# Where weight conversions stand behind attention, which queue stores a group's last piece, a lag ahead of a group, and a fill split unevenly

## The chip, the core and the metric

The kernel runs on one core of one Trainium2 chip. Its engines are TensorE (PE), VectorE (DVE), ScalarE (ACT), GpSimd (POOL) and SyncE (SP, which issues DMAs). The metric is the time of one execution on the device, in microseconds; less is better.

## What is computed

Three stages follow each other, all in float32. A gated linear attention runs over 4 batches, 8 heads, 768 steps and head size 48, with a complex decay a per step and channel. Its output rows go through a top-1 mixture of 8 experts, and the result through a dense gated stage.

```python
scale = min(mag, 0.999) / (mag + 1e-6)           # mag = |a|
for t in range(768):                             # S is complex, 48 x 48 per head
    S = (a[t] * scale[t]) * S + outer(k[t], v[t])
    y[t] = q[t] @ S.real
x = y as 3072 rows of 384
e = argmax(x @ w_gate); x = gate * (relu(x @ w1[e]) @ w2[e])
out = ((x @ v1) * (x @ v2)) @ w3 @ w_out         # v1, v2, w3, w_out arrive as float64
```

## The kernel before

**Attention in chunks.** The 768 steps are 3 groups of 4 chunks of 64 steps. One chunk of one pair of batches is a unit `u = (g, q, c)`, so a group has 8 units. Work of the attention runs as two streams of Python generators. `first()` (`Attn.elementwise`) goes through 24 pieces, on DVE and ACT for the most part: it takes the loaded decays, makes the prefix products of the decays (L891, L893) and multiplies q and k by them (`L923`, the last DVE operation of a piece). The result is stored to a scratch tensor in HBM, `qkd`, through POOL's queue. For the last piece of a group (pieces 9, 17 and 23) the first 64 lanes go through SP's queue and the other 64 through POOL's (L931, L932). `second()` (`Attn.groups`) reads `qkd` back by unit (tile `kk`, L1025 on SP), which can start only when the whole group has been stored.

**A unit.** `scores` transposes q and k on PE (L1009), copies the transposes with ACT (`qkT`, L1010), multiplies them (L1037) and masks the product with DVE (`at`, L1041). `outputs` makes the unit's 64 rows from the masked scores and the state (L1056, L1057), copies them (`xo`, L1060), and every two or four such tiles `route` computes the experts' logits and scatters the rows with POOL (L162). `chain` carries the state `W` in PSUM from unit to unit. Its first part multiplies the carried state by a permutation (L1094) and copies the sum as `z` with ACT (L1095); its second part adds the unit's outer products (L1101), scales the result with 8 ACT operations and one DVE operation into `cb` or `cc` (L1108, L1109) and with one more DVE operation in place (L1110). The next unit's L1094 needs both.

**The filling.** After each of the two parts of `chain` the generator calls `fill(cost)`, which takes steps of `scores`, `outputs` and `route` from a pool until their planned prices add up to `cost`. Prices are planned nanoseconds: 430 for four transposes, 680 for half the scores, 650 for two heads of outputs. Both calls use `FILL = 2600`.

**What sets the order.** `drive` interleaves the two streams by a planned clock for each: whichever is behind goes next, and what the second stream yields is multiplied by `GM = 0.85`. The order in which instructions are traced is their priority. A scheduler then plays the program with durations of its own, and lets an engine take a later instruction when the earlier one is not ready in that play. The order on each engine is fixed then; on the chip each engine takes its instructions strictly in that order. `tc.issue_after(x)` adds an edge: what is traced inside the block on x's engine stands behind x.

**The conversions.** The dense stage's last two matrices are float64. `Fuse` loads them (tile `fdr`, L291, on SP), splits each into a high and a low half on DVE and ACT (`halves`, L322 to L339) and multiplies them. While group 2's units are traced, one conversion step is taken after each `fill`, two after every third. They cover the 8 pieces of `w_out` and 4 of 8 blocks of `w3`. Each step is ordered behind `S.end` on S.end's engine, which is DVE: the newest L923, by then that of piece 23. Nothing in `_bound` binds a step to the attention's own operations of group 2.

**After the attention.** The product of the converted matrices stands on PE right behind the last outputs, the experts and the dense stage follow.

Of the kernel before, what the change touches and what calls it, by code (L numbers as in the profile page):

```python
# [14 lines left out]
AF = mybir.ActivationFunctionType  # L15
# [605 lines left out]
NH = 8  # L621
# [31 lines left out]
AHEAD = 3  # L653
WIN = 2
WARM = 8
REST = 3
ZB = 4
HP = 1000
# [27 lines left out]
class Fuse:  # L686
# [10 lines left out]
    def _singles(self):  # L697
        nc, S, wp = self.nc, self.S, self.wp
        self.wo = [wp.tile([128, NF, DM], F32R, tag=f"wo{x}", name=f"wo{x}") for x in "hl"]
        self.w3 = []  # L700

        def factor(f):
            return lambda: [x[:, f] for x in self.wo]

        def block(f, h):
            def place():
                if not h:
                    pool = wp if f % W3B == 0 else self.w2p
                    self.w3.append([pool.tile([128, NF, 128], F32R, tag=f"w3{x}{f % W3B}", name=f"w3{x}{f}") for x in "hl"])
                return [x.rearrange("p g c -> p (g c)")[:, h * 512 : (h + 1) * 512] for x in self.w3[f]]  # L710
            return place

        srcs = [S.w_out[f * 128 : (f + 1) * 128, :] for f in range(NF)]
        srcs += [S.w3[f, :, h * 512 : (h + 1) * 512] for f in range(NF) for h in range(2)]
        raws = ahead(doubles(self.w2p, nc.sync, 5), srcs, 4)
        first = [factor(f) for f in range(NF)] + [block(f, h) for f in range(W3B) for h in range(2)]
        rest = [block(f, h) for f in range(W3B, NF) for h in range(2)]
        for n, _ in enumerate(self._bound(halves(S, nc, raws, wp, first), lambda: [S.end])):
            self.ready = max((n - 1 - NF) // 2, 0)
            yield  # L720
        for n, _ in enumerate(self._bound(halves(S, nc, raws, wp, rest), lambda: S.gate)):
            self.ready = W3B + max((n - 1) // 2, 0)
            yield
# [67 lines left out]
class Attn:  # L791
# [33 lines left out]
    def elementwise(self, aside, factors):  # L825
# [84 lines left out]
        def keys(i):  # L910
            g, _, n = PAIRS[i][0]
            k = raw[i][:, :, 1]
            x, g0 = s2[i][:, 0], s2[i][:, 1]
            if i == LAST[g]:
                v.tensor_copy(S.xm[:, g], px[i][:, (n - 1) * D : n * D])
            v.tensor_tensor(out=x, in0=px[i], in1=g0, op=ALU.mult)
            yield 470
            v.tensor_tensor(out=k, in0=k, in1=td(g0), op=ALU.mult)
            yield 470
            v.scalar_tensor_tensor(out=k, in0=td(x), scalar=2.0, in1=k, op0=ALU.subtract, op1=ALU.mult, reverse0=True)  # L920
            yield 470
            self.qk[i] = o = self.qp.tile([128, TP, 2, 2, D], F32, tag="qk", name=f"qk{i}")
            S.end = v.tensor_tensor(out=o, in0=bc(P[i], 2, 2), in1=bc(raw[i], 2, 3), op=ALU.mult)  # L923
            yield 1740
            self.stored = self.qk.pop(i).rearrange("p t w r d -> p (t w r d)")
            at = 0
            for g, t, n in PAIRS[i]:
                dst = S.qkd[g].rearrange("q c h b t w e -> (q c h b) t (w e)")[:, t : t + n].rearrange("l t e -> l (t e)")
                src = self.stored[:, at * 2 * R2 : (at + n) * 2 * R2]
                if i == LAST[g]:  # L930
                    nc.sync.dma_start(dst[:64], src[:64])  # L931
                    done = nc.gpsimd.dma_start(dst[64:], src[64:])  # L932
                else:
                    done = nc.gpsimd.dma_start(dst, src)
                at += n
            with self.tc.issue_after(done.ins):
                aside(i)
            self.made = i + 1
# [89 lines left out]
    def scores(self, u, qk):  # L1028
        nc, S, st, pp = self.nc, self.S, self.st, self.pp
        yield from self.turn(u, qk)  # L1030
        qkT = self.qkT[u]
        nm = "%d%d%d" % u
        sc = pp.tile([128, NH, C], F32, tag="sc", name=f"sc{nm}")
        for h in range(NH):
            for i in range(2):
                t = slice(i * C, (i + 1) * C)
                nc.tensor.matmul(sc[t, h], qkT[:, 1, h, t], qkT[:, 0, h, t], start=True, stop=True)  # L1037
            if h % 4 == 3:
                if h == NH - 1:
                    at = st.tile([128, NH, C], F32, tag="at", name=f"at{nm}", bufs=2)  # L1040
                    nc.vector.tensor_tensor(out=at, in0=sc, in1=bc(S.mask, NH, 1), op=ALU.mult)  # L1041
                    self.at[u] = at
                yield 680

# [29 lines left out]
    def chain(self, u, ld):  # L1074

        nc, S, st = self.nc, self.S, self.st
        g, q, c = u
        nm = "%d%d%d" % u
        W = self.W[:R2, :, :HD]
        lanes = lambda x: x.rearrange("e k (l d) -> e k l d", d=D)  # L1080
        heads = lambda x: x.rearrange("e k (i h d) -> e k i h d", i=2, d=D)
        T = lambda r: self.T[:, r, q, c].rearrange("e (k l) -> e k l", k=2)
        v, kk = ld
        z = st.tile([R2, 2, HD], F32, tag="z", name=f"z{nm}", bufs=ZB)
        first = g == 0 and c == 0
        if first and q == 0:
            for k in range(2):
                nc.tensor.matmul(W[:, k], S.ident[:R2, :R2], self.ca[q][:, k], start=True, stop=True)
        elif c == 0:
            nc.scalar.copy(W, self.ca[q])  # L1090
        if not first:
            last = self.cc[q] if c == 0 else self.cb
            for k in range(2):
                nc.tensor.matmul(W[:, k], S.perm, last[:, k], start=False, stop=True, skip_group_check=True)  # L1094
            nc.scalar.copy(z, W)  # L1095
        self.pool.append(Item("outputs", self.outputs(u, v, heads(z)), lambda: u in self.at))
        yield 1300
        if g == NG - 1 and c == 3:
            return
        for h in range(NH):  # L1100
            nc.tensor.matmul(heads(W)[:, h // 4, :, h % 4], kk[:, h, 1], v[:, :, h], start=False, stop=True, skip_group_check=True)  # L1101
        if c < 3:
            self.cb = st.tile([R2, 2, HD], F32, tag="cb", name=f"cb{nm}", bufs=2)
            nb, na = self.cb, W
        else:
            nb, na = self.cc[q], self.ca[q]
        for l in range(NH):
            nc.scalar.activation(out=lanes(nb)[:, 0, l], in_=lanes(W)[:, 0, l], func=AF.Copy, scale=T(1)[:, 0, l : l + 1])  # L1108
        nc.vector.tensor_tensor(out=lanes(nb)[:, 1], in0=lanes(W)[:, 1], in1=T(1)[:, 1].unsqueeze(2).to_broadcast([R2, NH, D]), op=ALU.mult)  # L1109
        nc.vector.tensor_tensor(out=lanes(na), in0=lanes(W), in1=T(0).unsqueeze(3).to_broadcast([R2, 2, NH, D]), op=ALU.mult)  # L1110
        yield 750

    def fill(self, cost):
# [28 lines left out]
    def groups(self, route, side, free):  # L1142
# [5 lines left out]
        self.held = {}  # L1148
        self.pool, self.turns = [], 0
        self.spare = None  # L1150
        self.vz = st.tile([128, VBUF, 2, HD], F32, tag="vz", name="vz")
        nc.gpsimd.memset(self.vz, 0.0)
        for q in range(2):
# [9 lines left out]
        for n, u in enumerate(work):  # L1163
            g, q, c = u
            if q == 0 and c == 0:
                while self.pool and self.made <= LAST[g]:
                    yield self.fill(1)
                yield lambda: self.made > LAST[g]
                yield from self.ends(g)
                for x in work[n : n + 2]:  # L1170
                    if x not in ld:
                        ld[x] = self.loads(x)
                if g == NG - 1:
                    yield free
            if free() and not singles:
                singles = side.fuse.units
                side()
            self.pool.append(Item("scores", self.scores(u, ld[u][1])))
            for x in self.chain(u, ld.pop(u)):
                yield x  # L1180
                yield self.fill(S.fillcost)
                step += 1
                if singles:
                    for _ in range(1 + (step % 3 == 0)):
                        if side.fuse.ready < min(BEFORE, side.fuse.blocks + W3B):
                            next(singles, None)
            for x in work[n + 1 : n + 3]:
                if self.made > LAST[x[0]] and x not in ld:
                    ld[x] = self.loads(x)
# [138 lines left out]
            moe_again(tc, S)  # L1328


FILL = 2600
XB = 6
ZROWS = {i: [i] for i in range(NE)}
BEFORE = 6
# [3 lines left out]
def build(ctx, tc, S):  # L1338
# [4 lines left out]
    nc.scalar.preload_act_table_set("natural_log_exp_and_others")  # L1343
    make_consts(tc, S)
    attn_consts(tc, S)
    S.xbufs, S.fillcost = XB, FILL
    with ExitStack() as at:
        xr = tc.tile_pool(name="r", bufs=1, side="right")
        S.rpool = xr.__enter__()
# [99 lines left out]
```

## Time and profile before

| | us |
|---|---|
| three runs | 1002.07, 1007.34, 1010.77 (median 1007.34) |
| the profiled execution | 1002.09 |
| its span, first to last instruction | 999.8 |
| what lies around the span | 2.3 |

The profile is of one execution. In its rows an idle time in brackets is the time an engine stood still just before the instruction, and behind the arrow stands who ended it. Names ending in q (SPq, POOLq) are an engine's DMA queue.

### The profile page before, as it was taken

Reading aid. Unit: us, or ns where it says so; the run is one execution under the profiler, and the core shown is the slowest. Engines: PE = TensorE matmul, PEld = TensorE weight load, DVE = VectorE, ACT = ScalarE, POOL = GpSimd, SP = SyncE. Lnnn points to the kernel's source line nnn. Section 1 sums busy time; section 2 is a strip of 40 time slices with the busy share of each in tenths; the row PEclk is TensorE's granted clock in tenths of the full one; section 3 lists DMA queues with packets and bytes.
Section 4 is the critical chain, followed back from the end, with each engine's and each line's share of the span. In section 5 each row is a group of like instructions: output and inputs, shape, how many; then the busy total and the mean of one; then the engine's idle time right before and its main releaser. Section 6 shows DMA issues by size and latency. Waiting matters only on the chain. (4 is left out here: it accounts for less than half of the span.)

```text
span 999.8 us, 17051 instructions
## 1 busy us (share of the span) xinstructions
PE 896.6 (90%) x6386; PEld 764.5 (76%) x6386; DVE 603.0 (60%) x1313; ACT 495.6 (50%) x1113; POOL 141.8 (14%) x205
## 2 busy tenths in 40 slices
PE   4545699969997988999989999998999999999997
PEld 2212278758886767889979999997888888888886
DVE  5999999988967952476489995443232323232222
ACT  6557589967766764344456664443231313121211
POOL 5111100051020201000232201110000000000001
PEclk8677799977998989899999999999999999999999
DMA  6558696367747850453687745630000000000000
GB/s 221 180 184 280 213 312 213 98 217 235 229 148 255 255 190 26 144 182 102 201 212 182 203 125 135 137 74 2 1 9 25 11 22 9 24 8 25 9 24 32
DMA packets 94791, 128.75 MB, mean 129 GB/s; under 512 B 7680, under 2 KB 79280, under 8 KB 94704
## 3 DMA queue, kind: packets, MB, share of 16 engines
q1 hardware_dynamic: 80716, 82.22, 29.0%
q0 software_dynamic: 10880, 40.76, 11.5%
q10 hardware_dynamic: 3108, 4.65, 1.6%
q8 instruction: 51, 0.84, 0.3%
q14 instruction: 36, 0.29, 0.1%
HBM read 92.38 MB, written 35.22 MB: 128 GB/s over the span
## 5 line engine op out<-in xcount | busy, mean ns | idle before, releaser
L606 DVE TENSOR_TENSOR ab<-asb,pb 128x512 f32<-128x512 f32 x48 | 33.0, 687 | 188.2 <-PE pb L352 184.2
L345 ACT CAST h<-w 128x384 fp32r<-128x384 f32 x128 | 65.0, 514 | 94.4 <-PE ph L351 49.4
L346 DVE TENSOR_TENSOR l<-w,h 128x384 fp32r<-128x384 f32 x128 | 70.5, 554 | 62.4 <-ACT h L345 58.4
L601 ACT COPY asb<-pa 128x512 f32<-128x512 f32 x48 | 28.1, 586 | 121.2 <-PE pa L352 116.7
L839 PE MATMUL x<-s,ident 128*128 128x384 f32 x64 | 36.9, 716 | 46.3 <-ACT s L898 46.3
L345 ACT CAST gh<-ab 128x512 fp32r<-128x512 f32 x48 | 29.7, 619 | 95.0 <-DVE ab L606 95.0
L351 PE MATMUL py<-hl,h 128*128 128x432 f32 x192 | 69.9, 364 | 3.6 <-DVE hl L407 3.6
L350 PE MATMUL py<-hh,h 128*128 128x432 f32 x192 | 69.2, 360 | 1.9 <-ACT hh L406 1.9
L352 PE MATMUL ph<-xh,l 128*128 128x432 f32 x192 | 69.0, 360 | 0.0
L350 PE MATMUL ph<-xh,h 128*128 128x432 f32 x192 | 69.0, 360 | 0.0
L352 PE MATMUL py<-hh,l 128*128 128x432 f32 x192 | 68.9, 359 | 0.0
L351 PE MATMUL ph<-xl,h 128*128 128x432 f32 x192 | 68.9, 359 | 0.0
L1009 PE MATMUL tr<-ident,kk 128*96 128x128 f32 x384 | 60.0, 291 | 9.0 <-ACT qkT L1010 5.0
L570 POOL DMA_INDIRECT out<-ob,mdp x24 | 23.8, 992 | 305.3 <-DVE ob L569 163.5
L351 PE MATMUL po<-ol,gh 128*128 128x384 f32 x192 | 64.9, 338 | 0.0
L350 PE MATMUL po<-oh,gh 128*128 128x384 f32 x192 | 64.8, 337 | 0.0
L352 PE MATMUL po<-oh,gl 128*128 128x384 f32 x192 | 64.1, 338 | 0.0
L839 PEld LDWEIGHTS x<-s,ident 128*128 128x128 f32 x64 | 15.6, 269 | 63.1 <-ACT s L898 54.9
L891 DVE TENSOR_TENSOR pr<-cf,P 128x192 f32<-128x192 f32 (+1 forms) x159 | 62.1, 391 | 2.6
L1010 ACT COPY qkT<-tr 96x512 f32<-96x512 f32 x96 | 55.0, 601 | 13.3 <-PE tr L1009 12.7
L350 PE MATMUL pa<-yh,ah 128*128 128x512 f32 x144 | 57.1, 396 | 3.0 <-ACT yh L345 3.0
L351 PE MATMUL pb<-yl,bh 128*128 128x512 f32 x144 | 57.0, 396 | 0.0
(219 smaller groups left out, 2415.6 us busy)
## 6 DMA issues: line engine op xcount, KB each, us to landing
w<-in_w SPq DMA_DIRECT2D x128, 192.0 KB, 3.0
kk<-qkd SPq DMA_DIRECT2D x24, 768.0 KB, 9.2
qkd<-qk POOLq DMA_DIRECT2D x15, 768.0 KB, 5.5
fdr<-in_w SPq DMA_DIRECT2D x16, 512.0 KB, 5.4
qkr<-in_qk SPq DMA_DIRECT2D x16, 384.0 KB, 6.4
fdr<-in_v POOLq DMA_DIRECT2D x12, 512.0 KB, 6.5
qkd<-qk POOLq DMA_DIRECT2D x15, 384.0 KB, 5.0
a<-in_a SPq DMA_DIRECT2D x7, 768.0 KB, 7.3
```

The costliest lines, as they stand in the source:

```text
L345: nc.scalar.copy(H, src)
L346: nc.vector.tensor_tensor(out=L, in0=src, in1=H.bitcast(F32), op=ALU.subtract)
L350: nc.tensor.matmul(out, lh, rh, start=first, stop=False)
L351: nc.tensor.matmul(out, lh, rl, start=False, stop=False)
L352: return nc.tensor.matmul(out, ll, rh, start=False, stop=last)
L570: nc.gpsimd.indirect_dma_start(out=S.outv[j], out_offset=bass.IndirectOffsetOnAxis(ap=S.mdp[:, j, 0:1], axis=0), in_=ob, in_offset=None, b ...
L601: nc.scalar.copy(asb, pa)
L606: nc.vector.tensor_tensor(out=ab, in0=asb, in1=pb, op=ALU.mult)
L839: nc.tensor.matmul(p, S.ident, s[r], start=r == 0, stop=r == 1)
L891: v.tensor_tensor(out=pr, in0=cx, in1=bc(pv, 2, 2), op=ALU.mult)
L1009: nc.tensor.transpose(pt[:, h], qk[:, h0 + h, w], self.S.ident)
L1010: nc.scalar.copy(qkT[:, w, h0 : h0 + 4], pt)
```

## The change

Four things change, and all lie ahead of the experts.

- The conversion steps that are taken while group 2 is traced are ordered behind `S.beat`, not `S.end`. `chain` sets `S.beat` to its last ACT scaling (L1108) and its last DVE operation (L1110); `scores` replaces the DVE entry by its mask operation (L1041). A step is now held on ACT as well as on DVE.
- Both halves of the last piece of a group are stored through SP.
- At the start of groups 0 and 1 the second stream yields `LAG = 5000`, after the first loads of the group have been traced.
- The fill is 1500 behind the first part of `chain` and 3700 behind the second, in place of 2600 behind both. The sum is unchanged.

```diff
@@ constants
+FILL = 1500, 3700
+LAG = 5000
...
-FILL = 2600
@@ Fuse._singles
-        for n, _ in enumerate(self._bound(halves(S, nc, raws, wp, first), lambda: [S.end])):
+        for n, _ in enumerate(self._bound(halves(S, nc, raws, wp, first), lambda: S.beat)):
@@ Attn.elementwise, keys
                 if i == LAST[g]:
-                    nc.sync.dma_start(dst[:64], src[:64])
-                    done = nc.gpsimd.dma_start(dst[64:], src[64:])
+                    for l in (0, 64):
+                        done = nc.sync.dma_start(dst[l : l + 64], src[l : l + 64])
@@ Attn.scores
-                    nc.vector.tensor_tensor(out=at, in0=sc, in1=bc(S.mask, NH, 1), op=ALU.mult)
+                    S.beat = S.beat[:1] + [nc.vector.tensor_tensor(out=at, in0=sc, in1=bc(S.mask, NH, 1), op=ALU.mult)]
@@ Attn.chain
-            nc.scalar.activation(out=lanes(nb)[:, 0, l], in_=lanes(W)[:, 0, l], func=AF.Copy, scale=T(1)[:, 0, l : l + 1])
+            last = nc.scalar.activation(out=lanes(nb)[:, 0, l], in_=lanes(W)[:, 0, l], func=AF.Copy, scale=T(1)[:, 0, l : l + 1])
...
-        nc.vector.tensor_tensor(out=lanes(na), in0=lanes(W), in1=T(0).unsqueeze(3).to_broadcast([R2, 2, NH, D]), op=ALU.mult)
+        S.beat = [last, nc.vector.tensor_tensor(out=lanes(na), in0=lanes(W), in1=T(0).unsqueeze(3).to_broadcast([R2, 2, NH, D]), op=ALU.mult)]
@@ Attn.groups
                 if g == NG - 1:
                     yield free
+                else:
+                    yield LAG
...
-            for x in self.chain(u, ld.pop(u)):
+            for x, c in zip(self.chain(u, ld.pop(u)), FILL):
                 yield x
-                yield self.fill(S.fillcost)
+                yield self.fill(c)
```

## Rows read from the trace of the kernel before

**Rows 1.** Windows: engine busy us (instructions), granted clock share, DMA share, GB/s.
```profile
118.00:290.70 172.70, 159.96 (x2009) 128.39 (x2009) 160.03 (x384) 136.94 (x359) 29.89 (x31) 0.92 0.64 207
290.70:406.90 116.20, 100.96 (x1379) 83.15 (x1378) 65.64 (x171) 66.46 (x170) 13.81 (x12) 0.91 0.55 176
350.00:360.00 10.00, 6.89 (x54) 4.93 (x51) 7.11 (x20) 5.09 (x10) 0.00 (x0) 0.74 0.68 222
400.00:410.00 10.00, 9.12 (x83) 7.14 (x82) 0.00 (x0) 1.27 (x2) 0.07 (x1) 0.53 0.20 68
406.90:690.00 283.10, 275.03 (x1464) 261.84 (x1463) 189.69 (x396) 144.33 (x300) 45.67 (x47) 1.00 0.56 149
```

**Rows 2.** Timeline: last piece's last DVE operation, and the attention's last copied rows.
```profile
288.96 1.76 DVE L923 TENSOR_TENSOR qk<-P,qkr 128x1536 f32<-128x1536 f32 x1
...
406.97 0.48 ACT L1060 COPY xo<-y 128x384 f32<-128x384 f32 x1 [3.78 <-PE y L1057]
```

**Rows 3.** Waits of PE from 290.7 to 406.9: total us, times, longest.
```profile
PE W L1094 <- DVE W L1110: 6.8, 3, 3.1
PE tr L1009 <- ACT qkT L1010: 5.0, 2, 4.3
```

**Rows 4.** Timeline where the conversions begin: start, us, instruction, [idle before].
```profile
305.78 0.36 DVE L336 TENSOR_SCALAR fdm<-fdr 128x384 int32<-128x384 int32 x1 [5.01 <-DMA fdr<-in_w_out]
...
306.18 0.61 ACT L329 ACTIVATE fdm<-fdm,rebias 128x384 int32<-128x384 int32 x1 [6.06 <-DVE fdm L336]
...
307.65 0.56 ACT L1010 COPY qkT<-tr 96x512 f32<-96x512 f32 x1
...
308.26 1.09 PE L1009 MATMUL tr<-ident,kk 128*96 128x128 f32 x4 [4.32 <-ACT qkT L1010]
...
309.78 2.88 PE L1101 MATMUL W<-vz,kk 128*96 128x96 f32 x16 [0.42 <-ACT z L1095]
```

**Rows 5.** Timeline of one state update and the next, 343 to 361 us.
```profile
343.17 1.53 PE L1094 MATMUL W<-cb,perm 96*96 96x384 f32 x4
...
346.71 1.60 PE L1101 MATMUL W<-vz,kk 128*96 128x96 f32 x16 [0.52 <-ACT z L1095]
...
348.35 1.61 ACT L1108 ACTIVATE cb<-W,T 96x48 f32<-96x48 f32 x8 [0.72 <-PE W L1101]
...
350.83 0.54 DVE L1109 TENSOR_TENSOR cb<-W,T 96x384 f32<-96x384 f32 x1
...
354.68 0.43 DVE L337 TENSOR_SCALAR fdl<-fdr 128x512 uint16<-128x512 uint16 x1 [2.89 <-DMA fdr<-in_w]
355.02 0.95 DVE L1110 TENSOR_TENSOR W<-W,T 96x768 f32<-96x768 f32 x1
...
356.03 2.87 PE L1094 MATMUL W<-cb,perm 96*96 96x384 f32 x4 [3.11 <-DVE W L1110]
...
358.69 1.91 PE L1009 MATMUL tr<-ident,kk 128*96 128x128 f32 x8
```

**Rows 6.** Timeline of the last state update's reader.
```profile
399.51 2.84 PE L1094 MATMUL W<-cb,perm 96*96 96x384 f32 x4 [3.08 <-DVE W L1110]
```

**Rows 7.** ACT's group of copies z, 290.7 to 406.9: busy us, mean ns, idle before.
```profile
L1095 ACT COPY z<-W 96x768 f32<-96x768 f32 x10 | 7.9, 786 | 12.7 <-PE W L1094 8.1 <-DVE pos L155 4.5
```

**Rows 8.** Timeline of the stores that end groups 1 and 2, and group 1's first load.
```profile
213.13 0.47 SPq L931 DMA_DIRECT2D qkd<-qk  x1
...
215.40 1.16 POOL L934 DMA_DIRECT2D qkd<-qk  x2
...
216.54 0.55 POOL L932 DMA_DIRECT2D qkd<-qk  x1
...
220.25 5.84 SPq L1025 DMA_DIRECT2D kk<-qkd  x4
...
291.55 0.60 POOL L932 DMA_DIRECT2D qkd<-qk  x1
```

**Rows 9.** Longest wait of DVE from 118 to 290.7: total us, times, longest.
```profile
DVE s L835 <- ACT s L898: 2.9, 3, 2.3
```

More of the change, by code (lines that the diff above doesn't have):

```diff
@@ L1150, in groups @@
         self.spare = None
+        S.beat = []
         self.vz = st.tile([128, VBUF, 2, HD], F32, tag="vz", name="vz")
@@ L1345, in build @@
     attn_consts(tc, S)
-    S.xbufs, S.fillcost = XB, FILL
+    S.xbufs = XB
     with ExitStack() as at:
```

## The prediction

> **What bounds the kernel now.** I read the windows first, cut where the work changes hands. Up to 290.7 us, where the last piece's last product ends [rows 2], DVE is busy 160.0 of 172.7 us and PE 160.0 as well [rows 1]: the stream of pieces feeds the attention, and DVE, which works for both, sets the pace. From 290.7 to 406.9, where the attention's last rows are copied out [rows 2], DVE is busy 65.6 of 116.2 and ACT 66.5, PE 101.0 [rows 1]: here PE has the most to do, and stands still for 15.2 us. After that PE is busy 275.0 of 283.1 at full clock [rows 1], with nothing but its own work ahead of it. So a microsecond that the attention ends sooner should come out at the end nearly whole, and the question is what the change does to 118 to 406.9.
>
> The waits of PE in the last third of the attention are few and long: 6.8 us on the state's DVE operation in three waits, 5.0 us on the ACT copies of the transposes, 4.3 of it at once [rows 3]. I then went to the places in the timeline.
>
> **First stall, 300.8 to 308.3.** DVE stands 5.01 us for the first conversion's load; ACT stands 6.06 us behind it, since its next instruction is that conversion's second step. The copy of finished transposes stands behind the conversion on ACT and comes at 307.65, and PE gets on at 308.26 after 4.32 us [rows 4]. Nothing that PE needs was late; the conversion had only been put ahead in the two queues, and its data came late.
>
> **Second stall, 352.9 to 358.9.** The state update runs as it should up to L1109 at 350.83. Then DVE waits 2.89 us for another conversion's load, L1110 comes at 355.02, and PE stands 3.11 us [rows 5]. PE's granted clock in that slice is 0.74, so part of it ran at 1.2 GHz in place of 2.4 GHz [rows 1]: the four permutation matmuls then take 2.87 us against 1.53 shortly before [rows 5].
>
> **Third stall, 396.4 to 399.5.** PE stands 3.08 us for the last state update, here with no conversion in the way, because the filling has run out; the permutation then takes 2.84 us [rows 6], at a granted clock of 0.53 in that slice [rows 1].
>
> **The change part by part**, against the profiled 1002.1 us (span 999.8).
>
> *Conversions behind the beat.* Adds no instruction. The first step is traced after (2,0,0)'s first fill, and its edges go to the ACT and DVE operations of the unit before, so neither queue can meet it ahead of that unit's update. The first stall then goes: 4.3 us of standing, and the 2.88 us of outer products that followed it [rows 4] against 1.60 for the same sixteen [rows 5], 1.3 us: 5.6 us. The second: 3.1 us of standing, 1.3 us on the permutation (2.87 less 1.53), and, taking half of the 1.91 us of transposes as an estimate of what the lower clock cost, about 0.9: 5.3 us. I count 4 of it, for a step traced after a unit's first fill is bound to the update of the unit before and may still stand ahead of this one's; what helps it then is that steps come at an even pace and their loads, which SP issues when a buffer is free, get more time. Bounds: 0 and 5.3. What is late next is the work of PE itself. The price is that steps which ran early now come late: DVE has 50.6 us free in this stretch [rows 1], so they fit, but some of them fall between the last units' own operations. In the wake of a step, an update waits for at most what is ahead of it in the queue; I put 1 us for it, between 0 and the 2.9 us that one conversion held an update up for above [rows 5].
>
> *Fill 1500 and 3700.* After the first part PE needs to be kept busy until z is copied, 0.79 us [rows 7], plus handing over. After the second it has to cover 1.61 of ACT, 0.54 and 0.95 of DVE, 3.1 us in sequence [rows 5], and more where something stands between. Planned prices are near the real ones: eight transposes are planned at 860 ns and took 1.91 us at a low clock, about half that at the full one (an estimate) [rows 5]. So 2600 is too much for the first and too little for the second, and 1500 and 3700 fit. I credit the last update, where outputs that ran ahead of it will run behind it: 2.0 of 3.1 us of standing and 1.0 of the 1.3 us that the permutation lost [rows 5, 6], 3 us. Bounds: 0 and 4.4. Against it, z: a first fill of 1500 leaves some 0.7 us of margin, and where ACT is behind with other copies PE will wait. It already does so for 0.42 and 0.52 us [rows 4, 5]. With 0.4 us in each of some 8 units, I charge 3 us; bounds 0 and 4.2 (8 times 0.52). Before 290.7 such waits cost nothing while DVE is behind.
>
> *Store on SP.* The second half costs SP one more issue of 0.47 us [rows 8], with loads queued behind it that nobody is waiting for at that point. POOL loses an issue of 0.55 to 0.60 us. At group 2's end POOL's half went out at 291.55, 0.8 us after the product was ready at 290.72, behind POOL's scatters [rows 2, 8]; on SP it goes out about 0.5 us after the first half, so the load of kk can come some 0.3 us sooner. At group 1's end the gap is larger, 213.13 to 216.54, but the piece before has its own store on POOL at 215.40, which the load needs as well [rows 8]; at most 1.1 us, and DVE, not kk, is the bound there. I take 0.3; bounds -0.5 (the issue) and 1.4. The Trainium skill speaks against both forms: "DMA: Bandwidth & Descriptors", section "Rules for kernel authors", says that two transfers to disjoint halves of the partitions aren't worth it, since they share the same DMA engines and serialize, and asks for one transfer. By that rule moving a half is worth 0 and the split costs an issue; the sum would be 0.3 us smaller. The rows show that the difference lies in when POOL gets to the issue, which the rule doesn't treat.
>
> *Lag.* 5000 at 0.85 is 4.25 us of the second stream's planned clock, twice. It puts a group's first units behind more of the pieces on every engine, while the loads of kk are on their way. Where attention stood ahead of pieces and was held up, DVE gains: its longest wait on ACT is 2.3 us of 2.9 in all [rows 9]. Where the attention is merely moved back, its work is left for the stretch after 290.7, where PE is the bound. I take a gain of 1.7, between -8.5 (two lags, nothing gained by the pieces) and 12.7 (all of DVE's standing before 290.7 [rows 1]).
>
> Sum: 5.6 + 4 - 1 + 3 - 3 + 0.3 + 1.7 = 10.6 us off. The profiled execution would be 991.5. The median of the runs is 1007.34, 5.3 above it, and that is what I forecast against: 996.7, say 997.
>
> **The rivals.**
>
> *The pieces gain too.* If the lag and the shifted filling take the blocked ACT copies out of DVE's way, half of DVE's 12.7 us of standing before 290.7 [rows 1] comes on top: 6 us more, 990. For it: DVE's waits there end in ACT operations that stand behind attention's [rows 9]. Against it: they are spread thin.
>
> *The order holds but PE gains nothing.* The edges bind a step to the update before, not to this one, and the second stall stays (4 us lost); z waits at its bound (1.2 more) and late conversions delay an update by 2.9 (1.9 more): about 3.5 us gained, 1004. The change doing less than it says is this case as well: the scheduler's play had these loads early, and if it still does, only the first stall goes.
>
> *Slower: the attention held back.* The lags' 8.5 us of attention move behind 290.7 and PE, already the bound there, has them on top, while the pieces end no sooner because DVE was busy with pieces anyway. It decides if the last piece ends later than about 286 us: then the lag has bought less than half of what it cost. With only the 4.3 us of standing gone from the first stall, z at its bound (4.2) and one update held for 2.9, it comes to 8.5 - 4.3 + 4.2 + 2.9 = 11.3 us more: 1019. Against it: at 290.7 some of the attention was behind anyway, and filled the time that group 2's first load took.
>
> **How the numbers follow.** A measurement of this kernel can't tell a difference of under 1% (10 us) from none. My forecast has a chance of 0.54 and a range of its own of 988 to 1004, from the bounds of the conversions and the lag; a little over half of that lies below 997.3, so 0.31 faster and 0.23 the same. The pieces gaining too: 0.14, faster. No gain for PE: 0.19, the same. Held back: 0.13, of which 0.11 over 1%. Together 0.45 faster, 0.44 the same, 0.11 slower. The range of 985 to 1010 takes in the first three cases with their bounds and leaves out the last and the ends of the others, some 0.15.
>
> **What would show it.** Right: no idle time of DVE that a conversion's load ends before the attention is over; no wait of PE of over 2 us after 290.7; the attention's last copy at about 396 in place of 407; the granted clock over 0.9 in all slices of that stretch; waits of PE on z more and each under 0.6 us; POOL's last store gone and kk loaded some 0.3 us sooner after L923. Wrong: the last L923 later than 291; conversion loads still ending DVE's idle time ahead of an L1110; conversions crowded behind 395; or the gain used up before the experts' first matmuls, since I assume that all behind the attention just moves forward.

## The result and the profile after

| | before | after |
|---|---|---|
| median, us | 1009.06 | 1023.72 |
| runs, us | 1002.07 to 1014.38 (4) | 1015.87 to 1030.51 (4) |
| profiled execution, us | 1002.09 | 1015.87 |
| its span, us | 999.8 | 1013.7 |

The ratio is 1.0144, with a 95% interval of 1.0105 to 1.0183. The change made the kernel slower, where 997 was forecast. From L656 on, lines of the changed kernel are 2 higher (L1094 is L1096, L1095 z is L1097, L1101 is L1103, L1108 to L1110 are L1110 to L1112, L923 is L925).

The last piece's last product and the attention's last copied rows, in the timeline of the changed kernel (start, duration, engine, instruction, idle before it):

```profile
278.63 1.76 DVE L925 TENSOR_TENSOR qk<-P,qkr 128x1536 f32<-128x1536 f32 x1
...
419.40 0.48 ACT L1062 COPY xo<-y 128x384 f32<-128x384 f32 x1 [3.78 <-PE y L1059]
```

The pieces end 10.3 us sooner than in [rows 2], the attention 12.4 us later. What follows is as long as before: 594.3 us from that copy's start to the end of the span, against 592.8. So the loss lies between 118 and 419. Windows of the changed kernel (columns as in [rows 1]):

```profile
118.00:280.40 162.40, 139.61 (x1693) 110.49 (x1694) 153.20 (x364) 124.73 (x325) 19.51 (x25) 0.90 0.66 209
280.40:419.40 139.00, 124.63 (x1695) 103.15 (x1694) 74.99 (x190) 80.24 (x205) 15.59 (x14) 0.92 0.51 159
...
240.00:250.00 10.00, 6.29 (x46) 4.14 (x48) 9.93 (x32) 5.94 (x16) 0.63 (x1) 0.65 0.63 197
300.00:310.00 10.00, 10.00 (x149) 8.58 (x146) 4.99 (x12) 5.94 (x19) 0.00 (x0) 1.00 0.39 102
...
400.00:410.00 10.00, 9.12 (x89) 7.69 (x87) 1.54 (x8) 1.77 (x5) 1.94 (x2) 0.50 0.44 146
```

Where the first stall was (300 to 310), PE is now busy for the whole slice at full clock. But ahead of 280 it stands more: DVE is busy with pieces, and PE gets 139.6 of 162.4 us at a granted clock of 0.90. Waits (total, times, longest) of ACT and PE up to 280.4, then of PE and, for a conversion's load, of DVE behind it:

```profile
ACT s L900 <- DVE P L895: 17.7, 6, 5.1
...
PE tr L1011 <- DMA kk<-qkd: 5.9, 1, 5.9
...
PE W L1103 <- ACT z L1097: 3.0, 2, 1.9
...
PE W L1096 <- DVE W L1112: 6.0, 3, 2.7
PE rk L148 <- ACT xt L125: 2.3, 1, 2.3
PE y L1058 <- ACT z L1097: 1.8, 2, 0.9
...
DVE fdl L337 <- DMA fdr<-in_w: 7.1, 5, 2.7
```

The first of them leads to the place. L900 is a piece's first ACT operation, the square of its prefix products, which come from DVE. Two of its six waits, with the operations of the state update around them:

```profile
231.45 1.53 PE L1096 MATMUL W<-cc,perm 96*96 96x384 f32 x4
...
235.29 0.78 ACT L1097 COPY z<-W 96x768 f32<-96x768 f32 x1
...
236.12 2.79 PE L1103 MATMUL W<-vz,kk 128*96 128x96 f32 x16 [1.07 <-ACT z L1097]
...
241.70 0.84 ACT L900 ACTIVATE s<-P 128x768 f32<-128x768 f32 x1 [5.08 <-DVE P L895]
242.45 1.59 ACT L1110 ACTIVATE cb<-W,T 96x48 f32<-96x48 f32 x8
...
246.03 2.84 PE L1096 MATMUL W<-cb,perm 96*96 96x384 f32 x4 [2.86 <-DVE r L153]
...
248.91 0.80 ACT L1097 COPY z<-W 96x768 f32<-96x768 f32 x1 [2.04 <-PE W L1096]
...
253.06 0.84 ACT L900 ACTIVATE s<-P 128x768 f32<-128x768 f32 x1 [3.35 <-DVE P L895]
...
253.74 1.52 PE L1103 MATMUL W<-vz,kk 128*96 128x96 f32 x16
...
257.02 1.61 ACT L1110 ACTIVATE cb<-W,T 96x48 f32<-96x48 f32 x8
...
261.46 0.54 DVE L1111 TENSOR_TENSOR cb<-W,T 96x384 f32<-96x384 f32 x1
...
265.17 0.79 ACT L1097 COPY z<-W 96x768 f32<-96x768 f32 x1
```

The state's outer products are done at 238.9. The scaling L1110, which needs only them, begins at 242.45: it stands in ACT's queue behind a square that waits 5.08 us for a piece. PE runs out of other work meanwhile, and after 2.86 us of standing the next permutation takes 2.84 us against 1.53 at 231.45. It is the first stall of [rows 4] again, with a piece in the place of the conversion. The Trainium skill ("Perfetto Trace Analysis", section "Tensor Engine Instruction (MATMUL, LD_WEIGHTS)") says that ACT and DVE take their instructions strictly first in, first out; these rows agree.

That wait alone is not the loss, as the z copies of the kernel before show:

```profile
230.77 0.79 ACT L1095 COPY z<-W 96x768 f32<-96x768 f32 x1 [1.42 <-PE W L1094]
...
243.89 0.80 ACT L1095 COPY z<-W 96x768 f32<-96x768 f32 x1 [0.98 <-PE W L1094]
...
253.24 0.80 ACT L1095 COPY z<-W 96x768 f32<-96x768 f32 x1 [0.27 <-PE W L1094]
```

From group 1's first z to its second the two kernels take nearly the same, 13.6 and 13.1 us. The changed kernel falls behind by 4.5 us up to the first z and by 6.9 between the second and the third. The first z begins 2.3 us after its permutation ends at 232.98; ACT has a piece's operations to do meanwhile. After the second z the update stands in three queues: 4.0 us on PE behind outputs and transposes (249.71 to 253.74), 1.8 on ACT behind copies and a piece's operations (255.26 to 257.02), and 2.8 on DVE behind a piece's products and a mask (258.63 to 261.46). What each of them costs by itself was not measured.

The second place is group 2's tail:

```profile
369.72 1.62 ACT L1110 ACTIVATE cb<-W,T 96x48 f32<-96x48 f32 x8
...
373.06 0.43 DVE L337 TENSOR_SCALAR fdl<-fdr 128x512 uint16<-128x512 uint16 x1 [1.55 <-DMA fdr<-in_w]
...
374.73 0.54 DVE L1111 TENSOR_TENSOR cb<-W,T 96x384 f32<-96x384 f32 x1
375.31 0.96 DVE L1112 TENSOR_TENSOR W<-W,T 96x768 f32<-96x768 f32 x1
...
381.65 0.89 PE L1096 MATMUL W<-cb,perm 96*96 96x384 f32 x2
...
398.07 2.85 PE L1096 MATMUL W<-cb,perm 96*96 96x384 f32 x4
...
406.59 2.88 PE L1103 MATMUL W<-vz,kk 128*96 128x96 f32 x16
...
412.84 1.95 PE L1096 MATMUL W<-cb,perm 96*96 96x384 f32 x4 [2.73 <-DVE W L1112]
```

L1111 stands from 371.3, where ACT's scalings end, to 374.7: a conversion's load is 1.55 us of it, the rest is conversion operations and a mask ahead of it on DVE. The state is then ready at 376.3, and L1096 follows only at 381.65: transposes, scores, outputs and logits stand ahead of it on PE. Work of this kind is missing later: from 400 to 410 PE runs at a granted clock of 0.50, and the last permutation waits 2.73 us.

With the z copies as milestones: at the third unit of group 1 the changed kernel is 11.9 us behind the one before (265.17 against 253.24); by the first z of group 2's second pair it has made that up (365.15 against 365.91), and 12.7 us is what the conversions' order gives over the same stretch by itself (e2 below); the four z from there on take 49.7 us in place of 36.5. So +11.9 - 12.7 + 13.2 = +12.4 us.

### The profile page after: what moved, and what is told of

It is laid out like the page before. It is cut to its first block, busy times and chain, and to the rows that moved or that the text cites. A ratio compares the mean times of both kernels' runs of the same rounds, so it can differ in the third digit from the quotient of the medians.

```text
span 1013.7 us, 17044 instructions
## 1 busy us (share of the span) xinstructions
PE 896.1 (88%) x6386; PEld 765.9 (76%) x6386; DVE 607.5 (60%) x1313; ACT 497.8 (49%) x1113; POOL 134.5 (13%) x202
## 5 line engine op out<-in xcount | busy, mean ns | idle before, releaser
L1012 ACT COPY qkT<-tr 96x512 f32<-96x512 f32 x96 | 54.5, 590 | 18.1 <-PE tr L1011 17.6
L1058 PE MATMUL y<-z,qkT 96*64 96x48 f32 x704 | 54.1, 238 | 3.6 <-issue 1.9
```

The lines of the kernel that those rows point to most:

```text
L1012: nc.scalar.copy(qkT[:, w, h0 : h0 + 4], pt)
L1058: nc.tensor.matmul(y[ps, h], qkT[:, 0, h, ps], z[:, h // 4, i, h % 4], start=True, stop=False)
```

## The experiments

All are timed against the kernel before on the same chip; its median was 1001.5 to 1010.4 us from chip to chip, so ratios are compared. The columns: ratio with interval; ACT's waits for a piece's products from 118 to 280 us (5.3 to 6.5 of it ahead of 130 us in every kernel); start of z of group 1's third unit (the expectations call it the 13th z; it is the ninth); time from the first to the last of the four z of group 2's second pair (their "last three z"); last copy of xo.

| run | ratio | ACT waits | z | tail | last xo |
|---|---|---|---|---|---|
| before | 1 | 6.8 | 253.2 | 36.5 | 407.0 |
| the change | 1.0144 (1.0105 to 1.0183) | 17.7 | 265.2 | 49.7 | 419.4 |
| e1 lag alone | 0.9976 (0.9951 to 1.0002) | 9.5 | 255.3 | 34.0 | 405.6 |
| e2 conversions alone | 0.9913 (0.9885 to 0.9940) | 6.8 | 253.3 | 39.6 | 397.4 |
| e3 fill alone | 0.9971 (0.9941 to 1.0001) | 9.1 | 248.1 | 36.5 | 401.9 |
| e4 store alone | 1.0011 (0.9986 to 1.0036) | 7.7 | 253.4 | 36.5 | 404.4 |
| e5 all but lag | 0.9845 (0.9788 to 0.9901) | 7.9 | 246.2 | 39.9 | 386.1 |
| e6 all but fill | 0.9996 (0.9976 to 1.0016) | 9.4 | 254.9 | 39.8 | 401.4 |
| e7 all but conversions | 1.0121 (1.0069 to 1.0174) | 17.6 | 268.6 | 31.4 | 406.0 |
| e8 all but store | 1.0206 (1.0154 to 1.0259) | 17.4 | 272.1 | 51.6 | 427.5 |
| e9 lag at group 0 only | 1.0155 (1.0111 to 1.0198) | 17.2 | 267.1 | 56.5 | 423.3 |
| e10 lag at group 1 only | 0.9881 (0.9841 to 0.9921) | 8.1 | 249.4 | 39.1 | 394.3 |
| e11 lag 2500 | 0.9879 (0.9839 to 0.9919) | 8.4 | 252.9 | 35.0 | 390.1 |
| e12 lag -2500 | 1.0114 (1.0080 to 1.0149) | 6.4 | 255.0 | 56.4 | 415.9 |
| e13 update first | 0.9809 (0.9770 to 0.9848) | 9.4 | 246.5 | 33.0 | 390.7 |
| e14 update first, group 2 | 1.0031 (1.0002 to 1.0061) | 17.3 | 264.1 | 39.1 | 406.7 |
| e15 square behind update | 1.0148 (1.0070 to 1.0225) | 5.6 | 259.6 | 57.7 | 428.2 |
| e16 e13 without the lag | 0.9960 (0.9931 to 0.9988) | 15.0 | 249.1 | 39.3 | 406.2 |
| e17 lag 4000 | 1.0158 (1.0082 to 1.0235) | 17.4 | 268.7 | 47.1 | 417.2 |
| e18 lag 6000 | 0.9887 (0.9838 to 0.9936) | 7.3 | 251.0 | 36.4 | 393.0 |

**Each part alone.** Each run makes one of the four edits of the diff in the kernel before. Theory A: the lag holds the attention back. B: conversions behind the beat empty the end of the attention. C: the uneven fill does.

> The kernel before, with the lag alone. Theory A (the lag holds attention back): the last L923 comes 8 to 11 us sooner, copy T of group 1 some 6 us later than 224, and the time is 8 to 13 us longer. Theory B (conversions behind the beat empty the end of the attention) and theory C (the uneven fill does): no change within 4 us.

> The kernel before, with the conversions behind the beat alone. Theory A: the stall of PE at 303 to 308 goes and nothing else moves, 4 to 8 us shorter. Theory B: that stall goes, but from z of unit (2,1,0) to z of (2,1,3) it takes some 45 us or more in place of 36.5, and the time is 3 to 10 us longer. Theory C: 4 to 8 us shorter, as A.

> The kernel before, with 1500 and 3700 alone. Theories A and B: 0 to 4 us shorter. Theory C: the last three units of the attention have no filling left, 4 to 10 us longer, from z of (2,1,0) to z of (2,1,3) over 42 us.

> The kernel before, with both halves of a group's last store on SP alone. All theories: within 2 us of the kernel before; kk of group 2 is loaded 0.3 to 1 us sooner after the last L923.

None of the parts costs anything alone that is clear of noise. At 1002 us the four are worth -2.4, -8.7, -2.9 and +1.1 us, 12.9 off in sum, and together they are 1.44% slower. A, B and C all fall as theories of one edit; what is left is that edits spoil each other.

**Each part left out.** Each run is the change with one of the four edits undone. D: lag and uneven fill spoil each other's order. E: the loss is in conversions and fill together. F: in lag and conversions. G: the second issue on SP shifts the planned order.

> The changed kernel without the lag. Theory D (lag and uneven fill spoil each other's order): 985 to 993, 10 to 17 us under the kernel before, as the parts alone add up. Theory E (the loss lies in beat and fill together, at the end of the attention): 4 to 14 us over the kernel before, last three z over 45 us.

> The changed kernel with 2600 behind both parts. Theory D: 985 to 993. Theory E: 985 to 993 as well. Theory F (lag and beat spoil each other): 4 to 14 us over the kernel before.

> The changed kernel with the conversions behind S.end as before. Theory D: the loss stays and the beat's gain is missing, 1015 to 1030. Theories E and F: the loss is gone, 995 to 1003.

> The changed kernel with the last stores half on SP and half on POOL as before. Theories D, E and F: as the changed kernel, 1010 to 1022. Theory G (the second issue on SP shifts the planned order, and that is what loses): under 1000.

E and G fall with e5 and e8. Without the lag the change is 1.55% faster than the kernel before, so the lag costs 3.0%, some 30 us, inside the change. e6 came out between all its theories: the ratios of lag, conversions and store alone add up to 0.9900, and it measured 0.9996, so F holds in part. Those of lag, fill and store add up to 0.9958, and e7 measured 1.0121 (1012.6 us, where D had put down 1015 to 1030). So the lag costs 1.6% beside the fill and 1.0% beside the conversions. D stands, with part of F. The same place in e5, where lines are 1 lower:

```profile
239.41 1.61 ACT L1109 ACTIVATE cb<-W,T 96x48 f32<-96x48 f32 x8 [0.73 <-PE W L1102]
...
241.83 0.89 ACT L899 ACTIVATE s<-P 128x768 f32<-128x768 f32 x1
...
246.19 0.79 ACT L1096 COPY z<-W 96x768 f32<-96x768 f32 x1 [0.29 <-PE W L1095]
...
250.07 1.61 ACT L1109 ACTIVATE cb<-W,T 96x48 f32<-96x48 f32 x8 [0.73 <-PE W L1102]
...
253.91 0.85 ACT L899 ACTIVATE s<-P 128x768 f32<-128x768 f32 x1
```

The square stands behind the scaling and waits for nothing, and PE is busy 39.8 us of 230 to 270 at full clock, in place of 31.6 at 0.83.

**Which lag, and how much of it.** The edits: `elif g == 0:` or `elif g == 1:` in place of `else:` ahead of `yield LAG`, and `LAG = 2500`, `-2500`.

> The whole change, with the lag ahead of group 0 alone. Theory D1 (one of the two lags decides, the first: it moves group 1's updates behind the squares of pieces in ACT's fixed order): about as slow as the whole change, ratio to the kernel before 1.010 to 1.020, last z of group 1's first three units late (after 260 us). Rival D2 (each lag adds its own part, so that half of the 30 us stays): 0.997 to 1.003. Rival D3 (the second lag decides): near the change without any lag, 0.985.

> The whole change, with the lag ahead of group 1 alone. D1: near the change without any lag, 0.980 to 0.990, last xo before 392 us. D2: 0.997 to 1.003. D3: as slow as the whole change, 1.010 to 1.020.

> The whole change, with a lag of 2500 in place of 5000 ahead of both groups. If the loss grows with the planned time of the lag (30 us for 5000): about 1.000. If it is a matter of the order that comes about (updates behind squares of pieces): either near 0.985 or near 1.014, nothing between.

> The whole change, with -2500 in place of 5000: the second stream is put ahead of the pieces at groups 0 and 1. If what the lag costs is the attention's place behind the pieces, it is as good as no lag or better, 0.975 to 0.988. If the pieces then end later and hold the end of group 2's start up (DVE is busy with both until 290 us), it gives the gain back: 0.990 to 1.005, with the last piece after 290 us.

D1 holds: nearly all comes from group 0's lag (e10 is 0.4% above e5, with overlapping intervals, and its last copy of xo 2 us later than expected). Half the lag costs almost none of the loss. e12 missed both expected times: its group 1 is sound and its pieces end at 296.4, but its tail is as long as that of the slower kernels. There the state is ready at 366.29 and its permutation follows on PE at 376.75, behind filling.

**Is the order the cause?** In e13, e14 and e16 the update's own instructions are traced at a higher priority; in e15 a piece's ACT operations are bound behind the newest update. O: the order is the cause. P: the attention just stands further back, and the order goes along with it.

```diff
+near = lambda: self.tc.high_priority(HP) if COND else nullcontext()  # e14: g == 2; e13, e16: True
+with near():   # around L1096, L1097 and around L1103 to L1112
...
+with ExitStack() as order:                                           # e15
+  for x in getattr(S, "beat", []):
+    order.enter_context(self.tc.issue_after(x.ins))
   power(i - 1)
   weigh(i - 1)
```

> The whole change with the lag of 5000, and the state update's own instructions (permutation, z, outer products, scalings) traced at a higher priority, so that the scheduler takes them ahead of other work that is ready. Theory O (the loss is the order: updates queued behind pieces' squares in group 1 and behind filling in group 2): most of the 30 us comes back, ratio to the kernel before 0.985 to 0.997, ACT's wait for pieces' products under 10 us between 118 and 300, the 13th z before 257 us. Rival P (the attention simply stands further back, the order goes along with it): 1.008 to 1.018, the 13th z after 260 us.

> The same edit for group 2's units alone. Theory O: group 1 as slow as with the change (13th z near 265 us), the last three z within 42 us in place of 50: about 8 us come back, 1.003 to 1.009. Rival P: no difference, 1.012 to 1.018.

> The whole change with the lag of 5000, and each piece's square and its logarithm and exponential on ACT bound behind the newest traced update's scaling. Theory O: ACT's wait for pieces' products between 118 and 300 falls from 17.7 us to under 10, the 13th z comes before 257 us, and the ratio is 0.985 to 1.000. Rival P: the 13th z stays after 260 us and the ratio at 1.008 to 1.018.

> The change without the lag, with e13's edit. Theory O: nothing is left to gain in group 1 (ACT's wait for pieces' products is 7.9 us there), a few us in group 2: 0.975 to 0.986. Rival P: the same as without the edit, 0.980 to 0.990. A ratio over 0.995 would say that any edit of the order can cost 10 us, whatever it is meant to do.

With the lag in place e13 gets back all of the loss, a little more than O put down, against P: ACT's waits, the third z and the tail are those of the fast kernels. e14 does as O said for the tail alone, and leaves group 1 slow. Its tail, lines of the update 2 to 3 higher:

```profile
371.41 0.43 DVE L337 TENSOR_SCALAR fdl<-fdr 128x512 uint16<-128x512 uint16 x1 [1.27 <-DMA fdr<-in_w]
...
373.66 0.96 DVE L1115 TENSOR_TENSOR W<-W,T 96x768 f32<-96x768 f32 x1
...
374.68 2.87 PE L1098 MATMUL W<-cb,perm 96*96 96x384 f32 x4 [0.64 <-DVE W L1115]
```

The state is ready at 374.6 and the permutation begins at 374.68, no longer 5.4 us later. e15 takes ACT's wait away as O said, and is no faster: PE now stands 9.9 us at once for the routing's `oh` from DVE, the pieces end at 306.0, and the tail is long. To bind the pieces moved the stall. e16 missed both theories: it is 1.15% slower than e5 by the ratios, so the edit that heals the lagged kernel harms the other. By its own expectation that says that any edit of the order can cost 10 us, whatever it is meant to do. ACT's wait is back, 15.0 us, but group 1's third z is only 2.9 us behind that of e5, and the last copy of xo 20.1. So ACT's wait is no measure of the loss: e16 has it and is near the kernel before, e12 and e15 have the shortest of all and are slow. What e13 shows is that the lag's loss can be taken back by the order alone; which of the moved instructions did it stays open.

**A forecast from the order.** The order on an engine is fixed before the run and can be listed from the compiled kernel. Below, U is a run of scalings, p a piece's square, z a copy of z, as they follow each other on ACT from group 1's start (an update whose scalings are split shows as two U):

```
5000 (also 4000, e7, e8, e9)   p z p U z p U p z U p z U z
2500 (also 1500 to 3500)       p z U z p U p z U p z U z p U z U p z
6000                           z p U U z p U z U p z U p z U p z
none (also before, e10)        z p U z U p z U p z U p z U p z
```

> The whole change with a lag of 4000. Its updates and pieces' squares follow each other on ACT in the same sequence as at 5000. Theory O (the order decides): as slow as the change, 1.010 to 1.020, ACT's wait for pieces' products near 17 us, 13th z after 260. Rival (the length of the lag decides): between 2500 (0.988) and 5000 (1.014), 0.998 to 1.008.

> The whole change with a lag of 6000. Its sequence on ACT is not that of 5000 but near that without a lag. Theory O: faster than with 5000, 0.985 to 1.002, ACT's wait for pieces' products under 12 us, 13th z before 258. Rival (the length decides): slower than 5000, 1.015 to 1.025.

Both came out by the order and against the length: 4000 is as slow as 5000, and 6000 is 2.6% faster. This sequence does not rank all kernels, though: in the traces e16 has that of 6000 but for the split scaling, and is 0.9960 against 0.9887. The wait of ACT in e17, then in e18:

```profile
ACT s L900 <- DVE P L895: 17.4, 6, 5.1
```

```profile
ACT s L900 <- DVE P L895: 7.3, 3, 3.9
```

## Why the prediction was wrong

**The step that failed** is the lag's: "5000 at 0.85 is 4.25 us of the second stream's planned clock, twice", a gain of 1.7 within -8.5 and 12.7. The lag was priced by its planned length. Alone it is near that (2.4 us off, with the interval just reaching zero). Inside the change it costs 30 us, over three times the lower bound, because it changes which of two queued instructions stands first, and the length does not tell which: 2500 and 6000 cost 3 to 4 us against e5, 4000 and 5000 some 30. A second term was put at nothing: "Before 290.7 such waits cost nothing while DVE is behind". PE was as busy there as DVE (both 160.0 us [rows 1]). In the change PE stands 22.8 of the 162.4 us up to the pieces' end, against 12.7 of 172.7, and 11.9 us of attention are lost by the third unit although the pieces end sooner.

**The sum of parts** failed with it. The single prices came out within 3 us, but each was read from the order of the kernel before, and the edits make a new one.

**Conversions behind the beat**: 8.6 forecast, 8.7 measured alone, which is partly luck. In e2 the z copies gain 12.7 us up to the second pair of group 2, where the two stalls were credited with 9.6, and the tail takes 3.1 us longer, where 1 was charged. The first stall is gone. In the whole change the second is not, as was feared: loads still end DVE's idle time, 7.1 us in five waits for `in_w` and 3.2 in two for `in_w_out`, one of them ahead of the update above. That DVE waits is not itself the loss; e14's DVE waits in the same place and its kernel is 1% faster.

**Fill**: nothing forecast, 2.9 us off alone, with the interval just reaching zero. The credit was for the last update, but there PE still waits 3.05 us in e3, against 3.08, and the tail is 36.5 us as before; the third z of group 1 is 5.1 us sooner, ahead of 290.7, where nothing was counted. In the change the waits on z are up to 1.9 us ahead of 280 and 0.9 behind it, more than the 0.6 put down as the mark.

**Store**: 0.3 forecast, +1.1 alone with zero inside the interval. By the rule against halves in the Trainium skill ("DMA: Bandwidth & Descriptors", section "Rules for kernel authors") it is worth nothing; e4 agrees as far as its interval goes, 0.9986 to 1.0036, which doesn't tell 0 from 0.3 us. The 0.3 us were to come from an earlier load of kk. In e4 the first load of kk behind that store is issued at 295.26 us, as in the kernel before.

**What was to be seen.** Wrong: no wait of PE over 2 us (2.7), the clock over 0.9 in every slice (0.50 at 400), the last copy at 396 (419.4). Right: all behind the attention just moves.

**The rivals.** "The attention held back" had the right sign and place. Its price was again the lag's length, and its test was wrong: it was to decide if the last piece ended later than 286, and the piece ended at 280.4. Where updates stand back DVE has the pieces to do, so an early end of the pieces is no mark against this rival: of the kernels with the long wait of ACT, the change, e9 and e14 end them by 282.4, before e5 (283.9), though e8 ends them at 287.1.

**What beats both kernels**: the change without the lag (0.9845), or with it and with the update traced first (0.9809); their intervals overlap. **What stays open** is why the scheduler's play comes to these orders at 4000 and 5000; its own durations were not looked into. Open too is what each of the update's places in the three queues costs.

## What to carry to other kernels

Where an order is worked out ahead of the run, a knob has no price of its own: try it at several values, since its neighbours tell whether a result is the knob's or one order's. Find the operation that is carried from unit to unit, and read in each engine's queue what stands right ahead of it; an instruction there that waits for another stream is the first to suspect, whichever edit put it there. Try giving that operation its place explicitly, and time that too, since the same protection cost 1% in one of two kernels here.

## What the runs showed of the hardware

The granted clock makes a short stall dearer than it is. From 230 to 270 us PE is busy 31.6 us and granted 0.83; in e5 it is busy 39.8 us and granted 1.00. In the change the sixteen outer products take 2.79 us at 236.12, after PE had stood 1.07 us, and 1.52 at 253.74. From 400 to 410 us the granted clock is 0.50, the lower of the two levels: the permutation at 398.07 and the outer products at 406.59 take 2.85 and 2.88 us, against 1.53 and 1.60 for the same operations in [rows 5].
